# Sources of the first maxima and the order of the early expert rows in an attention and MoE kernel

## The chip, the cores and the metric

The kernel runs on one core of one Trainium2 chip. Times are device microseconds (us). A core has TensorE (PE in the profile, PEld its weight loads), VectorE (DVE), ScalarE (ACT), GpSimd (POOL) and SyncE (SP, here mostly the queue that issues transfers); GpSimd issues the indirect ones, gathers and scatters by a list of row numbers.

## The reference

Attention over 8 batches of 8 heads (576 positions, 64 per head) with a decay from a running sum of logarithms, then a mixture of 8 experts of which each row takes one:

```python
scores = scale * np.matmul(q, k.transpose(0, 1, 3, 2))
log_f = np.log(np.clip(f, 0.0001, 1.0))
cum = np.cumsum(log_f, axis=-1)
decay = cum[:, :, :, None] - cum[:, :, None, :]
scores = np.where(causal, -1000000000.0, scores + decay)
scores = scores - np.max(scores, axis=-1, keepdims=True)
attn = np.exp(scores)
attn = attn / (np.sum(attn, axis=-1, keepdims=True) + 1e-09)
x = np.matmul(attn, v)                      # then to rows of 512
...
logits = x @ w_gate
e_idx = np.argmax(logits, axis=1)
gate_w = softmax(logits)[e_idx]
eom = 1.0 / (1.0 + np.exp(-(x @ w_output_gate)))
out[e_idx == e] = gate_w * eom[:, e] * (np.maximum(x[e_idx == e] @ w1[e], 0.0) @ w2[e])
```

4608 rows of 512 go through W1 (512 x 1024) and W2 (1024 x 512) of their expert.

## The kernel before, in words

**Attention** is a program of steps, from -18 to 203, six steps for a unit of two heads; there are 32 units. A table, OFF, gives for each kind of work the step of a unit at which it is issued, and the engines run what they are given in that order. Before the exponent a unit needs the largest score of each row. maxsteps forms the scores of a block on TensorE, adds the decay there and reduces on VectorE into nR (L313); max_pair turns nR to half precision on ScalarE (mh, L374); max_turn transposes it on TensorE (mt, L379). The decay is a matmul of a few rows: Eq holds ones, Ek the running sum in three half-precision parts (few, L297). The running sum is made once for all 64 heads, in the prologue: a logarithm on ScalarE (L164), a scan and the parts on VectorE (tile d2, 64 partitions, one a head; the parts are cpc), and small DMAs that carry the parts of units 0 and 1 into Ek. wgs is the gate's weight, scaled on VectorE (L862). Vs holds V in a high and a low part, the low one by a subtraction (L143).

**Features.** The attention rows of two units each (u = 0 to 15 in feats) become x16 in two parts; DMA transposes bring them to xT (feats_turn, L568), from which TensorE makes the logits (route), and feats_out stores the rows in xbuf (L575, L580). route gives every row its place in its expert's list, and GpSimd scatters the row's number there, a tile of 128 rows at a time (tbl, L680): five scatters for the odd batches, four for the even.

**Experts.** The first 384 rows of experts 0 and 1 are taken early, those of expert 1 from batches 0 to 5: SyncE reads the row numbers (ids, L727), GpSimd gathers the rows (xg, L731), DMA transposes make xT (L737). up is xT times W1 (hp, L952), 8 pieces of 12 matmuls with 384 columns; down is the result times W2 (y, L980 to L982), a tile of 128 rows at a time, and each tile is scattered into the output by GpSimd (L985). The weights come as single-precision pieces (w1r, L693; w2r, L710) that are split into two parts, w1h on ScalarE and w1l on VectorE or GpSimd (L700), w2h and w2l likewise. Where attention ends TensorE does up and down of expert 0's early rows, batch 7's logits between the second and third tile of down, then expert 1's early rows (x1), then late rows and experts 2 to 7.

The semaphores of SyncE's transfers are eight that are used in turn.

Of the kernel before, what the change touches and what calls it, by code (L numbers as in the profile page):

```python
# [9 lines left out]
F32 = mybir.dt.float32  # L10
# [44 lines left out]
OFF = {'lead': 2, 'crow': -16, 'clear': 32, 'clearstep': 12, 'prefill': -15, 'fetch': -22, 'spread': -21, 'end': 204, 'max': (-15, -13, -11, -10), 'pair': -8, 'mturn': -7, 'rows': -6, 'put': -6, 'rscore': 2, 'rexp': 3, 'first': -9, 'av': ((6, 8, 8), (10, 10, 10)), 'fetch_v': -23, 'v': ((-15, -9, -17), (-9, 0, -12)), 'feats0': 20, 'feats1': 22, 'fturn': 21, 'fturnstep': 1, 'fout': 33, 'route': 46, 'rank': 6, 'w1r': [169, 170, 171, 175, 176, 178, 180, 181], 'w1': [174, 175, 178, 179, 181, 182, 200, 202], 'w2r': [183, 184, 184, 186, 186, 187], 'hold': (160, 196), 'ids1': 192, 'gather': 172, 'ids': 7, 'gturn': 6, 'route_last': 200, 'nsum': (9, 11), 'nrec': (10, 12), 'nx': (10, 13), 'nrest': (11, 14), 'mv': ['xr', 'v0', 'sm'], 'same': (-4, 0), 'begin': -18, 'pd': [7], 'turn': {'v0': 0, 'v1': 0, 'f0': 0, 'f1': 1, 'w': 1}, 'wg': -4, 'fetch_v/1': -15, 'dve': [172, 173, 181, 183, 184, 185, 186, 187, 189, 190], 'w1pool': [0, 1, 2, 3, 4, 5, 6, 7], 'order': 'nrec tick reduce rows v1 put spread fetch_v fout feats1 scores feats0 tick v0 max fetch exps mturn tick rexp nsum extra rscore av maxrest route fturn pair nx tick nrest', 'epool': [6, 7]}  # L55
# [11 lines left out]
def _attn_moe(ctx, tc, qk, vm, f, wg, w1, w2, out):  # L67
# [87 lines left out]
    def prologue():  # L155
# [34 lines left out]
    for t in (pick, negm, negt):  # L190
        nc.gpsimd.memset(t, 0.0)
    for i in range(HU):
        for h in range(2):
            def select(t, sign, op, fill):
# [92 lines left out]
    def maxsteps(u):  # L287
# [471 lines left out]
    def attention():  # L759
# [7 lines left out]
        for s in range(OFF["begin"], OFF["end"]):  # L767
# [82 lines left out]
            def extras():  # L850
# [5 lines left out]
                if s == OFF["ids1"]:  # L856
                    gather_ids(ar, tbl[NT:NT + EARLY], ET, 0, (st["ids"],))
# [40 lines left out]
        return [c for c in chains]  # L898
# [110 lines left out]
    with tc.manual_schedule(engines=ENGINES):  # L1009
# [37 lines left out]
        for _ in range(11):  # L1047
            next(chain)
# [127 lines left out]
```

## Time and profile before

| | us |
|---|---|
| timed, median of 3 | 799.69 |
| the 3 runs | 798.03 to 801.85 |
| profiled execution, own time | 792.31 |
| its span, first to last instruction | 790.6 |
| TensorE busy in the span | 753.9 (95%) |
| GpSimd, VectorE, ScalarE busy | 462.8, 355.0, 343.2 |
| mean granted TensorE clock | 0.99 |

All rows come from the one profiled execution. Busy time overlaps between engines. A timeline's row is an instruction, or a run of like ones (x8: eight), with the idle time of its engine before it and what ended that. For SyncE's queue a row's time is that of issuing, waits included, not of the transfer.

### The profile page before, as it was taken

What the parts mean: (1) busy time and instruction counts of PE and PEld (TensorE: products, weight loads), DVE (VectorE), ACT (ScalarE), POOL (GpSimd) and SP (SyncE); (2) the same over time, 40 slices, a digit from 0 to 9 for tenths busy, and PEclk for the clock granted to TensorE, in tenths of its full rate; (3) what the DMA queues carried; (4) which work ended last, traced back from release to release, by engine and by line L of the source; (5) the groups of instructions that cost most, each with busy time, mean ns of one, the idle gap of its engine ahead of it and who ended that gap; (6) DMA issues with size and microseconds to landing.
All of it is one profiled execution on the core that took longest, in us unless ns stands there. A gap on an engine that the chain in (4) does not pass through costs nothing. (4 is left out here: it accounts for less than half of the span.)

```text
span 790.6 us, 21337 instructions
## 1 busy us (share of the span) xinstructions
PE 753.9 (95%) x8677; PEld 493.5 (62%) x8695; DVE 355.0 (45%) x909; ACT 343.2 (43%) x821; POOL 462.8 (59%) x488
## 2 busy tenths in 40 slices
PE   4899999999989999899799999999999999999996
PEld 1577777777767777675355667556465574664752
DVE  7566687777767878976350142002011020120210
ACT  2556666465646564664331424333333333333211
POOL 9567669687867877656154538464564654736001
PEclk9999999999999999999989999999999999999999
DMA  5446678778867778599959739456562594452001
GB/s 189 135 126 149 178 186 184 185 174 172 159 166 165 174 193 184 115 217 187 209 114 259 201 86 260 130 167 152 174 162 75 175 210 129 139 118 80 11 13 45
DMA packets 136245, 121.49 MB, mean 154 GB/s; under 512 B 95342, under 2 KB 104974, under 8 KB 136144
## 3 DMA queue, kind: packets, MB, share of 16 engines
q1 hardware_dynamic: 128592, 101.18, 54.4%
q0 software_dynamic: 7552, 18.92, 7.7%
q8 instruction: 69, 1.13, 0.7%
q14 instruction: 32, 0.26, 0.1%
HBM read 81.63 MB, written 20.48 MB: 129 GB/s over the span
## 5 line engine op out<-in xcount | busy, mean ns | idle before, releaser
L415 POOL TENSOR_TENSOR plo<-p 128x512 f16<-128x512 f32 x167 | 173.4, 1054 | 62.7 <-ACT p L413 39.5
L962 DVE SCALAR_TENSOR_TENSOR hl<-hp,hh 128x384 f16<-128x384 f32 (+1 forms) x128 | 60.7, 491 | 304.2 <-ACT hh L961 179.9
L952 PE MATMUL hp<-xT,w1h 128*128 128x256 f16 (+1 forms) x1024 | 190.2, 302 | 5.4 <-DMA xT<-xg 5.4
L413 ACT ACTIVATE p<-sc 128x512 f32<-128x512 f32 x192 | 110.3, 593 | 67.3 <-PE sc L285 61.4
L285 PE MATMUL sc<-qk 64*128 64x64 f32 (+5 forms) x642 | 135.0, 476 | 0.0
L952 PEld LDWEIGHTS <-w1h 128*128 128x128 f16 x1024 | 100.6, 98 | 46.7 <-issue 7.5
L985 POOL DMA_INDIRECT out_dram<-ys,ids x40 | 40.2, 1005 | 144.0 <-ACT ys L984 87.6
L980 PE MATMUL y<-w2h,hh 128*128 128x512 f16 x320 | 121.9, 381 | 1.8 <-ACT w2h L912 1.8
L952 PE MATMUL hp<-xT,w1l 128*128 128x384 f16 (+1 forms) x512 | 122.9, 301 | 0.0
L982 PE MATMUL y<-w2h,hl 128*128 128x512 f16 x320 | 121.9, 381 | 0.9
L981 PE MATMUL y<-w2l,hh 128*128 128x512 bf16 x302 | 115.2, 382 | 0.3 <-DVE w2l L913 0.3
L961 ACT ACTIVATE hh<-hp 128x384 f16<-128x384 f32 (+1 forms) x128 | 50.8, 436 | 131.2 <-PE hp L952 120.1
L328 DVE CUSTOM_DVE_ANT_0 spare<-mx,wide 128x512 bf16<-128x512 f32 (+1 forms) x120 | 74.9, 624 | 43.1 <-PE mx L285 38.4
L984 ACT ACTIVATE ys<-y,ids 128x512 f32<-128x512 f32 x40 | 27.5, 687 | 152.6 <-issue 99.1
L700 POOL TENSOR_TENSOR w1l<-w1r,w1h 128x512 bf16<-128x512 f32 x54 | 61.8, 1158 | 50.5 <-ACT w1h L699 50.4
L285 PEld LDWEIGHTS <-pick 64*128 64x128 bf16 (+1 forms) x1152 | 59.2, 96 | 41.9 <-issue 24.6
L313 DVE TENSOR_REDUCE nR<-mx 128x1 f32<-128x576 f32 (+3 forms) x95 | 60.5, 637 | 29.1 <-PE mx L285 27.3
L489 PE MATMUL av<-Vs,p 128*128 128x65 f16 x640 | 70.4, 195 | 2.9 <-ACT xr L536 2.2
L285 PE MATMUL mx<-qk 64*64 64x64 bf16 (+2 forms) x374 | 59.3, 310 | 13.7 <-DMA qk<-in_qk_dram 8.6
L491 PE MATMUL av<-Vs,plo 128*128 128x65 f16 x640 | 69.3, 193 | 0.5 <-issue 0.5
L490 PE MATMUL av<-Vs,p 128*128 128x64 bf16 x640 | 69.8, 196 | 0.0
L952 PEld LDWEIGHTS <-w1l 128*128 128x128 bf16 x512 | 50.4, 98 | 20.1 <-issue 1.0
(166 smaller groups left out, 1430.8 us busy)
## 6 DMA issues: line engine op xcount, KB each, us to landing
qk<-in_qk_dram SPq DMA_DIRECT2D x32, 576.0 KB
w1r<-in_w_dram SPq DMA_DIRECT2D x64, 256.0 KB
w2r<-in_w_dram SPq DMA_DIRECT2D x64, 256.0 KB
v<-in_vm_dram SPq DMA_DIRECT2D x16, 576.0 KB
wide<-crow SPq DMA_DIRECT2D x30, 288.0 KB
xbuf<-x SPq DMA_DIRECT2D x16, 512.0 KB
Eq<-mts SPq DMA_DIRECT2D x64, 0.1 KB
xbuf<-x SPq DMA_DIRECT2D x16, 64.0 KB
```

What stands on the lines that cost most here:

```text
L285: nc.tensor.matmul(dst(i), w(i), x(i), start=start, stop=stop)
L328: nc.vector.tensor_tensor_reduce(out=spare[:, 0:n], in0=part(m, i, o, n), in1=t["wide"][:, i * S:i * S + n], scale=1.0, scalar=-3e38, op0= ...
L413: nc.scalar.activation(out=f32, in_=src, func=AF.Exp, scale=0.125)
L415: ins = eng.tensor_tensor(lo, f32, upper(f32), op=ALU.subtract)
L489: nc.tensor.matmul(dst, ph, vv[:, 0:W], start=kc == 0, stop=False)
L490: nc.tensor.matmul(dst[:, 0:D], ph, vv[:, W:].bitcast(BF16), start=False, stop=False)
L491: nc.tensor.matmul(dst, pl, vv[:, 0:W], start=False, stop=kc == qc)
L700: ins = (eng or nc.vector).tensor_tensor(l, raw, h, op=ALU.subtract)
L952: nc.tensor.matmul(m[:, 0:(t1 - t0) * P], w[:, k], xT[:, t0:t1, k // 2, j, k % 2], start=k == 0 and i == 0, stop=k == ND - 1 and i == 2)
L980: nc.tensor.matmul(y, hh[:, fc, sl], wh, start=fc == 0, stop=False)
L981: nc.tensor.matmul(y, hh[:, fc, sl], wl, start=False, stop=False)
L982: nc.tensor.matmul(y, hl[:, fc, sl], wh, start=False, stop=fc == NF - 1)
```

## The change

In the start: for units 0 and 1 the decay's stationary operand is a column of the identity, spread, and its moving operand the first part of the running sums of all heads (cpa, 128 partitions, of which the upper 64 are zeroed), so that a column picks its head. Ek of units 0 and 1 is filled with ones by ScalarE, two memsets go to VectorE, the loads have another order on SyncE, the low part of V (V's first two subtractions) and the gate's scaling stand at later steps.

Where attention ends: the features of u = 15 are transposed on TensorE and copied from PSUM (feats_swap); batch 7's logits come right behind up, its ranks behind the first tile of down; the numbers of expert 1's rows are read after all scatters of batch 5, and batch 6's scatters stand ahead of expert 1's gathers; expert 2's gathers stand between splits of W1.

```diff
-OFF = { ... 'v': ((-15, -9, -17), (-9, 0, -12)), ... 'wg': -4, ... }
+OFF = { ... 'v': ((-15, -9, -5), (-9, 0, -3)), ... 'wg': 20, ... }
...
@@ -79,10 +79,12 @@
     d1 = ar.tile([P, 2048], F32, name="d1", tag="x")[0:B * H]
-    d2 = ar.tile([P, 2048], F32, name="d2", tag="x")[0:B * H]
+    d2f = ar.tile([P, 2048], F32, name="d2", tag="x")
+    d2 = d2f[0:B * H]
     ft, lf, zr = [d1[:, j * S:(j + 1) * S] for j in range(3)]
     cum, rem = [d2[:, j * S:(j + 1) * S] for j in range(2)]
     cpc = d2[:, 2 * S:2 * S + 3 * S // 2].bitcast(F16).rearrange("p (c s) -> p c s", c=3)
+    cpa = d2f[:, 2 * S:2 * S + S // 2].bitcast(F16)
     raw = {}
...
@@ -112,7 +114,7 @@
         return slice(i * D, (i + 1) * D)
     def blank(i, eng=nc.gpsimd):
-        if i != 1:
+        if i > 1:
             eng.memset(Eks[i], 1.0)
         eng.memset(Eqs[i], 0.0)
...
@@ -156,9 +158,11 @@
         nc.sync.dma_start(ft, f)
         fetch(0)
-        nc.sync.dma_start(wg32, wg)
-        fetch_v(0)
+        fetch(1)
         nc.vector.memset(zr, 0.0)
+        for i in range(2):
+            nc.scalar.activation(out=Eks[i].rearrange("p (n q) -> p n q", q=D), func=AF.Copy, scale=0.0, bias=1.0,
+                                 in_=identh[:, 0:D].unsqueeze(1).broadcast_to([P, S // D, D]))
         blank(0, nc.vector)
         nc.vector.tensor_scalar(ft, ft, 1e-4, 1.0, op0=ALU.max, op1=ALU.min)
         nc.scalar.activation(lf, ft, AF.Ln)
...
@@ -173,8 +177,9 @@
             for u in range(2):
                 nc.sync.dma_start(Eks[u].rearrange("(h d) s -> h d s", h=HU)[:, i, :],
                                   cpc[u * HU:(u + 1) * HU, i, :])
-        fetch(1)
+        fetch_v(0)
         fetch(2)
+        nc.sync.dma_start(wg32, wg)
     order = actx.enter_context(ExitStack())
...
@@ -182,23 +187,18 @@
     wg32 = cp.tile([P, 4, 2 * E], F32, name="wg32")
     late = cp.tile([P, EE], F32, name="late")
+    apart = cp.tile([P, 1], F32, name="apart")
     identh = cp.tile([P, P], F16, name="identh")
-    nc.gpsimd.memset(Eks[1], 1.0)
     make_identity(nc, identh)
+    nc.gpsimd.memset(cpa[B * H:], 0.0)
...
+        (nc.gpsimd if t is negt else nc.vector).memset(t, 0.0)
...
@@ -294,13 +294,20 @@
         def few(x, i, sl):
-            return x[i * D:i * D + 1 if u < 2 else (i + 1) * D - 1, sl]
+            return x[i * D:(i + 1) * D - 1, sl]
+        def own(i, n):
+            return identh[:, HU * u + i:HU * u + i + 1].broadcast_to([P, n])
         def block(m, o, c):
             n = (c + 1) * P
             q = slice(c * P, n)
-            decay = [(lambda i: part(m, i, o, n), lambda i: few(t["Eq"], i, q), lambda i: few(t["Ek"], i, slice(0, n)),
-                      False, False)]
+            if u < 2:
+                decay = [(lambda i: part(m, i, o, n), lambda i: own(i, P), lambda i: cpa[:, 0:n], False, False)]
+            else:
+                decay = [(lambda i: part(m, i, o, n), lambda i: few(t["Eq"], i, q),
+                          lambda i: few(t["Ek"], i, slice(0, n)), False, False)]
...
@@ -356,10 +363,10 @@
             m = mtile().rearrange("p b n -> p (b n)")[:, 0:S]
             q = slice(SM, S)
             for sl in (slice(0, SM), q):
-                own = sl is q
+                last = sl is not q
                 heads([(lambda i: m[rows(i), sl], lambda i: Qu[rows(i), q], lambda i: Ku[rows(i), sl], True, False),
-                       (lambda i: m[rows(i), sl], lambda i: few(t["Eq"], i, q), lambda i: few(t["Ek"], i, sl),
-                        False, not own)])
+                       (lambda i: m[rows(i), sl], lambda i: own(i, SR) if u < 2 else few(t["Eq"], i, q),
+                        lambda i: cpa[:, sl] if u < 2 else few(t["Ek"], i, sl), False, last)])
...
@@ -853,8 +860,6 @@
                 for e in range(EE):
                     if s == OFF["hold"][e]:
                         hold_early(e)
-                if s == OFF["ids1"]:
-                    gather_ids(ar, tbl[NT:NT + EARLY], ET, 0, (st["ids"],))
                 if s == OFF["gather"]:
                     chains.append(early_gather())
@@ -895,7 +900,15 @@
             for name in OFF["order"].split():
                 todo[name]()
             assert set(todo) == set(OFF["order"].split())
-        return [c for c in chains]
+        for c in chains[:-1]:
+            n = len(scatters)
+            while next(c, c) is not c:
+                now[0] += 1
+                if len(scatters) > n:
+                    nc.gpsimd.memset(apart, 0.0)
+                    n = len(scatters)
+        gather_ids(ar, tbl[NT:NT + EARLY], ET, 0, (st["ids"],))
+        return chains[-1:]
...
@@ -1006,6 +1019,18 @@
     x1 = (st["ids"], m2.tile([P, CT, 2, 2, DM // P // 2, P], F16, name="xT", bufs=1))
     first = [(0, ET)]
     late_rows = [(ET, CT)]
+    def feats_swap(u, t0, copy):
+        xT, x16 = xTs[u]
+        t1 = min(t0 + 2, NTB)
+        n = (t1 - t0) * 4
+        m = pm.tile([P, DM], F32, name="y", bufs=2).bitcast(F16).rearrange("p (c n) -> p c n", n=P)
+        src = x16[:, t0:t1].rearrange("p t j (k n) -> p (t j k) n", n=P)
+        for c in range(n):
+            nc.tensor.transpose(m[:, c], src[:, c], identh)
+        copy(out=xT[:, t0:t1].rearrange("p t j k n -> p (t j k) n"), in_=m[:, 0:n])
     with tc.manual_schedule(engines=ENGINES):
         for t in range(ET):
             gather_rows(x1, t, EARLY_B[1] * S, (ET + t) % CT)
@@ -1021,9 +1046,9 @@
             if fc == 1:
                 for part in range(2):
                     feats(NQ - 1, part)
-                    for t in ((0,), (2, 4))[part]:
-                        feats_turn(NQ - 1, t)
                 feats_out(NQ - 1)
+            if fc in (4, 5, 6):
+                feats_swap(NQ - 1, 2 * (fc - 4), nc.scalar.copy if fc == 5 else nc.vector.tensor_copy)
         W1r = [fetch_w1(m2, w1[1], fc, 8) for fc in range(NF)]
         for t in range(ET):
             gather_turn(x1, t, (ET + t) % CT)
@@ -1038,14 +1063,13 @@
             if len(raws) < NF:
                 raws.append(fetch_w2(w2[e], len(raws)))
-        down(W2, x, h, 0, 2)
-        more_w1(2, nc.vector)
         for _ in range(9):
             next(chain)
-        more_w1(2, nc.vector)
-        down(W2, x, h, 2, ET)
+        down(W2, x, h, 0, 1)
         for _ in range(11):
             next(chain)
+        more_w1(4, nc.vector)
+        down(W2, x, h, 1, ET)
         for t, _ in enumerate(chain):
             if t % 2:
                 more_w1(1, nc.gpsimd)
...
@@ -1067,12 +1091,12 @@
         x2 = next_ids(ar, EE)
         W1r = [fetch_w1(m2, w1[EE], fc, 8) for fc in range(NF)]
         W2r = [fetch_w2(w2[EE], fc) for fc in range(6)]
-        for t in range(CT):
-            gather_rows(x2, t)
         down(W2b, x1, h, 0, ET)
         W1c = []
         for fc in range(NF):
             up_split(up_products(W1, x, late_rows, fc), h, late_rows, fc)
+            if fc < CT:
+                gather_rows(x2, fc)
             W1c.append(split_w1(ar, W1r[fc], NF, nc.gpsimd))
         x2 = next_turns(ar, x2)
         down(W2, x, h, ET, CT)
```

VectorE, from the first reduction of the program. Vs is the low part of V, nR the maxima of unit 0, mts the transposed maxima. Before:

```order
L313 TENSOR_REDUCE nR<-mx 128x2
L313 TENSOR_REDUCE nR<-av 128x1 x4
L143 TENSOR_TENSOR Vs_90<-v_153,Vs_90 128x9x64
L313 TENSOR_REDUCE nR<-sc 128x1 x2
L313 TENSOR_REDUCE nR<-mx 128x1
```

After:

```order
L320 TENSOR_REDUCE nR<-mx 128x2
L320 TENSOR_REDUCE nR<-av 128x1 x4
L320 TENSOR_REDUCE nR<-sc 128x1 x2
L320 TENSOR_REDUCE nR<-mx 128x1
L394 COPY mts<-mt 9x128
```

The subtraction has left the middle of unit 0's reductions; it stands behind those of unit 1 now.

GpSimd, where attention ends. tbl with pi_7856 (after: pi_7858) are batch 5's scatters, with pi_8660 (pi_8663) batch 6's; xg are expert 1's gathers. Before:

```order
L700 TENSOR_TENSOR w1l_8592<-w1r_8142,w1h_8591 128x512
L680 DMA tbl_202<-rec_222,pi_7856 36864x2 x2
L731 DMA xg_226<-xbuf_73,ids_7804 128x1024 x3
L680 DMA tbl_202<-rec_222,pi_8660 36864x2 x4
L985 DMA out_0_dram<-ys_8923,ids_7801 4608x512
```

After:

```order
L700 TENSOR_TENSOR w1l_8593<-w1r_8144,w1h_8592 128x512
L687 DMA tbl_204<-rec_224,pi_7858 36864x2
L908 MEMSET apart_101 128x1
L687 DMA tbl_204<-rec_224,pi_7858 36864x2
L687 DMA tbl_204<-rec_224,pi_8663 36864x2 x4
L738 DMA xg_228<-xbuf_73,ids_7806 128x1024 x3
L998 DMA out_0_dram<-ys_9004,ids_7803 4608x512
```

The gathers have moved behind batch 6's scatters, and a small memset stands between the last two of batch 5.

SyncE there, with the semaphores that each instruction waits for (DMAHW0 to 7 are those of SyncE's own transfers, DMASW those of GpSimd's). Before:

```order
L568 DMA_TRANSPOSE xT_8334<-x_8335 128x8x128 [waits DMAHW3_49,DVE_49]
L727 DMA ids<-tbl 128x3x2 [waits DMAHW4_49,DMASW3_49]
L568 DMA_TRANSPOSE xT_8334<-x_8335 128x4x128 [waits DMAHW5_49,DVE_49]
L575 DMA xbuf<-x_8335 128x4x512 [waits DMAHW6_49]
L580 DMA xbuf<-x_8335 64x512 [waits DMAHW7_49]
L580 DMA xbuf<-x_8335 64x512 [waits DMAHW0_49]
L710 DMA w2r<-in_w_dram 128x512 [waits DMAHW1_49,DVE_49]
L710 DMA w2r<-in_w_dram 128x512 [waits DMAHW2_49,DVE_49]
L568 DMA_TRANSPOSE xT_8739<-x_8740 128x8x128 [waits DMAHW3_49,DVE_49,PE_49]
L568 DMA_TRANSPOSE xT_8739<-x_8740 128x8x128 [waits DMAHW4_49,DVE_49]
L568 DMA_TRANSPOSE xT_8739<-x_8740 128x4x128 [waits DMAHW5_49,DVE_49]
L575 DMA xbuf<-x_8740 128x4x512 [waits DMAHW6_49]
```

After:

```order
L575 DMA_TRANSPOSE xT_8336<-x_8337 128x4x128 [waits DMAHW4_49,DVE_49]
L582 DMA xbuf<-x_8337 128x4x512 [waits DMAHW5_49]
L587 DMA xbuf<-x_8337 64x512 [waits DMAHW6_49]
L587 DMA xbuf<-x_8337 64x512 [waits DMAHW7_49]
L717 DMA w2r<-in_w_dram 128x512 [waits DMAHW0_49,DVE_49]
L734 DMA ids<-tbl 128x3x2 [waits DMAHW1_49,DMASW5_49]
L717 DMA w2r<-in_w_dram 128x512 [waits DMAHW2_49,DVE_49]
L582 DMA xbuf<-x_8743 128x4x512 [waits DMAHW3_49,DVE_49]
L587 DMA xbuf<-x_8743 64x512 [waits DMAHW4_49,DVE_49]
L587 DMA xbuf<-x_8743 64x512 [waits DMAHW5_49]
L700 DMA w1r<-in_w_dram 128x512 [waits DMAHW6_49,Pool_49]
```

The read of ids has moved from between the transposes of u = 14 to between the last two pieces of W2, and waits for a later scatter; the three transposes of xT_8739 (u = 15) are gone.

## Rows read from the trace of the kernel before

**Rows 1.** Windows: span, busy (count) of PE, PEld, DVE, ACT, POOL; granted clock, DMA, GB/s.

```profile
0.00:20.00 20.00, 9.70 (x75) 3.67 (x76) 14.87 (x31) 4.92 (x7) 18.05 (x54) 1.00 0.58 189
...
420.00:780.00 360.00, 359.21 (x2177) 214.24 (x2191) 56.96 (x124) 115.86 (x244) 175.21 (x161) 1.00 0.50 139
```

**Rows 2.** Timeline of VectorE, first 24 us: start, us, engine, line, operation [idle before].

```profile
9.69 1.23 DVE L313 TENSOR_REDUCE nR<-mx 128x2 f32<-128x1024 f32 x1 [0.26 <-PE mx L285]
...
11.28 1.42 DVE L313 TENSOR_REDUCE nR<-av 128x1 f32<-128x384 f32 x4 [0.37 <-PE av L285]
...
12.62 0.75 DVE L143 TENSOR_TENSOR Vs<-v,Vs 128x576 bf16<-128x576 f32 x1
...
19.62 0.18 DVE L862 TENSOR_SCALAR wgs<-wg 128x64 f16<-128x64 f32 x1
...
19.98 0.68 DVE L313 TENSOR_REDUCE nR<-mx 128x2 f32<-128x512 f32 x1
```

**Rows 3.** Timeline of ScalarE, the same stretch.

```profile
0.83 1.28 ACT L164 ACT_TABLE_LOAD   x1 [0.83 <-PEq L1164]
...
4.48 0.68 ACT L164 ACTIVATE d<-d 64x576 f32<-64x576 f32 x1 [2.37 <-DVE d L163]
...
14.73 0.21 ACT L374 ACTIVATE mh<-nR 128x9 f16<-128x9 f32 x1 [5.50 <-DVE nR L313]
```

**Rows 4.** Timeline of TensorE, start of the program.

```profile
8.74 0.61 PE L285 MATMUL mx<-Ek,Eq 1*128 1x512 f16 x2 [2.58 <-DMA Ek<-d]
...
20.71 0.63 PE L285 MATMUL mx<-qk 64*64 64x512 bf16 x2 [1.65 <-DVE nR L313]
...
28.05 0.22 PE L379 MATMUL mt<-identh,mh 128*9 128x128 f16 x1
```

**Rows 5.** Timeline of TensorE where attention has ended.

```profile
376.85 0.38 PE L980 MATMUL y<-w2h,hh 128*128 128x512 f16 x1 [1.83 <-ACT w2h L912]
...
396.61 0.80 PE L952 MATMUL hp<-xT,w1h 128*128 128x384 f16 x2 [5.25 <-DMA xT<-xg]
...
402.19 0.49 PE L952 MATMUL hp<-xT,w1h 128*128 128x384 f16 x2
```

**Rows 6.** Windows of 5 us over the same place, columns as in group 1.

```profile
375.00:380.00 5.00, 2.82 (x9) 1.09 (x9) 1.20 (x2) 1.68 (x3) 0.83 (x1) 0.81 1.22 172
380.00:385.00 5.00, 5.00 (x25) 2.20 (x24) 0.00 (x0) 0.00 (x0) 0.17 (x1) 0.84 0.99 104
...
395.00:400.00 5.00, 3.39 (x11) 1.61 (x12) 0.00 (x0) 0.07 (x1) 4.10 (x5) 0.52 0.92 301
```

**Rows 7.** Timeline of SyncE's queue (SP), 340 to 445 us.

```profile
363.58 4.49 SPq L568 DMA_TRANSPOSE xT<-x  x3
...
370.53 17.06 SPq L693 DMA_DIRECT2D w1r<-in_w_dram  x8
...
387.69 5.77 SPq L737 DMA_TRANSPOSE xT<-xg  x3
...
410.96 0.89 SPq L727 DMA_DIRECT2D ids<-tbl  x2
```

**Rows 8.** Timeline of GpSimd (POOL), 340 to 445 us.

```profile
354.95 2.27 POOL L700 TENSOR_TENSOR w1l<-w1r,w1h 128x512 bf16<-128x512 f32 x2 [3.69 <-ACT w1h L699]
...
361.69 1.48 POOL L680 DMA_INDIRECT tbl<-rec,pi  x1 [4.47 <-DMA ids<-tbl]
...
364.76 1.54 POOL L731 DMA_INDIRECT xg<-xbuf,ids  x1 [0.30 <-issue]
...
391.00 0.99 POOL L985 DMA_INDIRECT out_dram<-ys,ids  x1 [10.84 <-issue]
...
396.66 0.98 POOL L680 DMA_INDIRECT tbl<-rec,pi  x1 [0.30 <-issue]
...
403.88 0.98 POOL L680 DMA_INDIRECT tbl<-rec,pi  x1 [0.17 <-issue]
...
413.73 1.04 POOL L731 DMA_INDIRECT xg<-xbuf,ids  x1 [6.57 <-DMA ids<-tbl]
```

More of the change, by code (lines that the diff above doesn't have):

```diff
@@ L51 @@
 EE = 2
-OFF = {'lead': 2, 'crow': -16, 'clear': 32, 'clearstep': 12, 'prefill': -15, 'fetch': -22, 'spread': -21, 'end': 204, 'max': (-15, -13, -11, -10), 'pair': -8, 'mturn': -7, 'rows': -6, 'put': -6, 'rscore': 2, 'rexp': 3, 'first': -9, 'av': ((6, 8, 8), (10, 10, 10)), 'fetch_v': -23, 'v': ((-15, -9, -17), (-9, 0, -12)), 'feats0': 20, 'feats1': 22, 'fturn': 21, 'fturnstep': 1, 'fout': 33, 'route': 46, 'rank': 6, 'w1r': [169, 170, 171, 175, 176, 178, 180, 181], 'w1': [174, 175, 178, 179, 181, 182, 200, 202], 'w2r': [183, 184, 184, 186, 186, 187], 'hold': (160, 196), 'ids1': 192, 'gather': 172, 'ids': 7, 'gturn': 6, 'route_last': 200, 'nsum': (9, 11), 'nrec': (10, 12), 'nx': (10, 13), 'nrest': (11, 14), 'mv': ['xr', 'v0', 'sm'], 'same': (-4, 0), 'begin': -18, 'pd': [7], 'turn': {'v0': 0, 'v1': 0, 'f0': 0, 'f1': 1, 'w': 1}, 'wg': -4, 'fetch_v/1': -15, 'dve': [172, 173, 181, 183, 184, 185, 186, 187, 189, 190], 'w1pool': [0, 1, 2, 3, 4, 5, 6, 7], 'order': 'nrec tick reduce rows v1 put spread fetch_v fout feats1 scores feats0 tick v0 max fetch exps mturn tick rexp nsum extra rscore av maxrest route fturn pair nx tick nrest', 'epool': [6, 7]}
+OFF = {'lead': 2, 'crow': -16, 'clear': 32, 'clearstep': 12, 'prefill': -15, 'fetch': -22, 'spread': -21, 'end': 204, 'max': (-15, -13, -11, -10), 'pair': -8, 'mturn': -7, 'rows': -6, 'put': -6, 'rscore': 2, 'rexp': 3, 'first': -9, 'av': ((6, 8, 8), (10, 10, 10)), 'fetch_v': -23, 'v': ((-15, -9, -5), (-9, 0, -3)), 'feats0': 20, 'feats1': 22, 'fturn': 21, 'fturnstep': 1, 'fout': 33, 'route': 46, 'rank': 6, 'w1r': [169, 170, 171, 175, 176, 178, 180, 181], 'w1': [174, 175, 178, 179, 181, 182, 200, 202], 'w2r': [183, 184, 184, 186, 186, 187], 'hold': (160, 196), 'ids1': 192, 'gather': 172, 'ids': 7, 'gturn': 6, 'route_last': 200, 'nsum': (9, 11), 'nrec': (10, 12), 'nx': (10, 13), 'nrest': (11, 14), 'mv': ['xr', 'v0', 'sm'], 'same': (-4, 0), 'begin': -18, 'pd': [7], 'turn': {'v0': 0, 'v1': 0, 'f0': 0, 'f1': 1, 'w': 1}, 'wg': 20, 'fetch_v/1': -15, 'dve': [172, 173, 181, 183, 184, 185, 186, 187, 189, 190], 'w1pool': [0, 1, 2, 3, 4, 5, 6, 7], 'order': 'nrec tick reduce rows v1 put spread fetch_v fout feats1 scores feats0 tick v0 max fetch exps mturn tick rexp nsum extra rscore av maxrest route fturn pair nx tick nrest', 'epool': [6, 7]}
 MV = OFF['mv']
@@ L184, in _attn_moe @@
     late = cp.tile([P, EE], F32, name="late")
+    apart = cp.tile([P, 1], F32, name="apart")
     identh = cp.tile([P, P], F16, name="identh")
-    nc.gpsimd.memset(Eks[1], 1.0)
     make_identity(nc, identh)
+    nc.gpsimd.memset(cpa[B * H:], 0.0)
     pick, negm, negt = [cp.tile([P, 2, P], BF16, name=n) for n in ("pick", "negm", "negt")]
[L190 to L194, printed above, removed]
+    for t, sign, op, fill in ((pick, 1, ALU.not_equal, 1.0), (negm, 1, ALU.is_ge, -8e9), (negt, -1, ALU.is_ge, -8e9)):
+        (nc.gpsimd if t is negt else nc.vector).memset(t, 0.0)
+        for i in range(HU):
+            for h in range(2):
                 nc.gpsimd.affine_select(out=t[rows(i), h], in_=t[rows(i), h], pattern=[[-sign, P]], compare_op=op,
                                         fill=fill, base=sign * h * D, channel_multiplier=sign)
-            select(pick, 1, ALU.not_equal, 1.0)
-            select(negm, 1, ALU.is_ge, -8e9)
-            select(negt, -1, ALU.is_ge, -8e9)
     prologue()
```

## The prediction

> **What bounds the kernel now.** I read the busy times by engine first, then windows over the whole core, then the timeline of TensorE for its idle stretches. TensorE is the bound nearly everywhere: from 420 to 780 us it is busy 359.21 of 360 us [rows 1], so nothing that the change moves there can pay unless it starts earlier. Two places are left. In the first 20 us TensorE is busy 9.70 us [rows 1], since the decay and the first maxima pass through one chain from engine to engine. [...] The reader is to see that these two hold all that can be gained, and that everything else counts only by delaying them.
>
> The sum is made against the profiled execution, 792.31 us; the timed median, 799.69, lies 7.4 above it, and I carry that difference over.
>
> **The start.** The headline edit takes the decay of the first two units' maxima out of Ek. TensorE's first such matmuls stand at 8.74 us behind a wait of 2.58 for the DMA into Ek [rows 4]. That wait is mostly not on the path: the reduction which reads them, at 9.69, waited for TensorE only 0.26 us; VectorE had been busy till then with the sums that make the decay [rows 2]. So at most 0.26 goes. Against it stands a new load on ScalarE: two fills of Ek ahead of the logarithm, which I price at 0.68 each, as the logarithm over the same 576 columns, and an activation table more, 1.28 [rows 3]. From 0.83 that is 1.28 + 2 x 0.68 + 1.28, the logarithm at 4.75 instead of 4.48: 0.27 later. The first part comes out at nothing, and 0.7 worse if the first fill waits for the identity that GpSimd builds.
>
> What does pay is what leaves VectorE's chain. The subtraction for V, 0.75 at 12.62, stood between two reductions of the first unit, of which one waited 0.37 for TensorE [rows 2]; it goes behind both units. I count 0.7 and 0.37. The gate's two scalings, from 19.62 to 19.98, 0.36 us, stood before the reduction for which TensorE waits 1.65 at 20.71 [rows 2, 4]; they go to step 20, where TensorE is the bound. The sum is -1.4. Below it the term ends at -2.9 (the whole wait of 1.65 and the pieces that ScalarE's 14.73 ends [rows 3] with it), above it at +0.3, if a load on SyncE's queue that now stands behind other ones (V and the gate) is late.
>
> **The end of attention.** Three moves work on one chain there, that of expert 1's early rows: numbers (ids1), gathers, transposes, then TensorE.
>
> What holds it now: the scatters of batch 5 end late since scatter 4 waits 4.47 us for SyncE's read of the numbers [rows 8], and expert 1's transposes stand behind eight reads of W1, 17.06 us long, at 387.69 [rows 7]; xT is ready at 396.61, 8.9 us after the first of these is issued. The length of the 17.06 is from semaphores that must come back: each transfer waits for the one eight before it, and three of those are transposes of the last features (4.49 us of the queue, at 363.58).
>
> Now scatter 4 needs no wait: it follows the split at 354.95 + 2.27 = 357.2, scatter 5 at 358.7 (1.48 each). Its landing isn't in the trace. Batch 7's five took from 396.66 to 410.96, 14.3 us or 2.86 each, and the last 7.1 from its own issue [rows 7, 8]. Two from 357.2 make 362.9, 7.1 from 358.7 makes 365.8: I take these as ends, with the whole 14.3 as a far end (a rival). A read of numbers takes 2.8 (410.96 to 413.73). So batch 6's four scatters start at 365.7 to 368.6, are issued 1.5 apart, and at 2.86 each have landed by 377 to 380. The gathers follow at about 372 to 375 and land with or behind them. SyncE reaches the W1 reads at 366 to 370, and now without the three transposes among those waited for; the last three wait for the features' stores, which I expect behind the scatters, at 377 to 380. Then 8.9 us for the transposes: xT at 386 to 389. If nothing but the 4.49 is saved it is 392.1; if nothing at all, 396.6. I take 390, near the first.
>
> TensorE itself: it would be done at 396.61 - 5.25 = 391.36. The wait of 1.83 for W2's last piece goes, because matmuls of 128 columns, logits and ranks now stand between up and down and the three transposes that shared the DMA engines with that piece are gone; cover lost, its 1.83 stays. With no pause before it the clock doesn't fall: 375 to 385 had 0.81 and 0.84 granted [rows 6], 0.95 + 0.80 = 1.75. To this come 20 transposes of 128 columns. The one transpose of the trace takes 0.22 at the low clock [rows 4], 4.4 in all; a matmul at 420 to 780 takes 359.21/2177 = 0.165 with 256 columns or more [rows 1], so 0.08 each, 1.6 in all, which I take as the nearer row. Their copies lie on VectorE and ScalarE, which are half idle there (1.20 and 1.68 busy of 5 us [rows 6]). TensorE is free at 391.36 - 1.83 - 1.75 + 1.6 = 389.4.
>
> [...]
>
> So expert 1's up starts at 390 instead of 396.61: -6.6. From 396.61 to 402.19 it ran at the low level (0.52 granted from 395 to 400; two matmuls took 0.80, then 0.49 [rows 5, 6]); 5.58 us of work at half speed, 2.8 lost. Without a wait of several microseconds before it that is back: -2.8.
>
> The added cost is GpSimd's. The splits of W1 4 to 7 for expert 1 stand there behind the out scatters and among batch 7's scatters, 396.66 to 404.9 now [rows 8]. If up starts 6.6 earlier these must too. An out scatter waited 10.84 for the one before (at 391.00); with the other scatters earlier in the queue I expect most of it gone, and count +1.0 (0 to +4).
>
> Expert 2's gathers, placed between splits, cost nothing by the 359.21 of 360: TensorE covers them; uncovered, a gather's 1.54 would show once [rows 8]. The two memsets that VectorE takes over at the very start lie in ScalarE's wait of 2.37 for the numbers f [rows 3]; uncovered they delay the whole chain by their own few tenths.
>
> Sum: -1.4 - 6.6 - 2.8 + 1.0 = -9.8: 782.5 in the profiled execution's terms, 789.9 or 790.0 beside the median.
>
> **The rivals.**
> 1. *The numbers earlier, the rows not.* The eight W1 reads keep their 17.06 and xT comes at 396.6 as now; the pause stays and with it the low clock. For it: SyncE's queue is in order, the same DMA engines carry scatters, W1 and rows (104 GB/s at 380 to 385 [rows 6]). Against: three of the eight transfers waited for are gone. Only -1.4 is left: 798.3.
> 2. *GpSimd's chain of outs takes over.* Each out still waits some 10 us for the former, batch 7's scatters stay at 396.66, the last splits end at 407 as now. Up reaches its eighth piece at 390 + 7 x 1.98 = 403.9 (12 matmuls a piece at the 0.165 above) and waits 3.2 there, 1.0 of which is counted; that the last two splits (2.27) follow scatter 403.88 [rows 8] is where the 407 is from. 782.5 + 2.2, beside the median 792.1.
> 3. *Slower: SyncE stands at the read of expert 1's numbers.* The read waits for batch 5's last scatter and everything behind it on SyncE (the last piece of W2, the stores, W1, the transposes) waits along. If that scatter lands 14.3 after its issue, at 373.0, the numbers are there at 375.8, and W1's reads begin 5.3 after 370.53; 17.06 and 8.9 behind make xT 401.9. With the start's gain lost to the logarithm (+0.3): 797.9, beside the median 805.3. It decides from a landing later than 370.5 on, 11.8 after the issue. For it speaks the 14.3; against it that those were five scatters and here there are two.
> 4. *The transposes on TensorE are dear.* Each takes the 0.22 of [rows 4], 4.4 in all, and the clock stays low while they run, so the 1.75 isn't won: TensorE is free at 391.36 - 1.83 + 4.4 = 393.9, 3.9 after the 390 of the sum: 793.8. For it: the only row of a transpose; against it: that row stands among half-clock matmuls. [...]
>
> **How the numbers follow.** Forecast 0.56, rival 1 0.17, rival 2 0.15, rival 3 0.07, rival 4 0.05. No change is within 0.5% of 799.69, 4.0 us, which is about what a measurement of this kernel can tell: 795.7 to 803.7. The forecast and rivals 2 and 4 are faster, 0.76; rival 1 is the same, 0.17; rival 3 slower, 0.07. The forecast's own range is 785.5 to 793 (start -2.9 to +0.3, xT from 386 to 392, splits 0 to 4, not all at one end). To leave out no more than 2 in 10, the range goes over rivals 2 and 4 to rival 1: 785.0 to 798.5.
>
> **What would show it.** Right: the pause before expert 1's up under 2 us, no stretch of half clock behind it, TensorE's first exponent matmuls 1 to 2 us earlier, the transposes under 2 us in sum. Wrong at the start: VectorE's first reduction later than 10.0. Rival 1: the read of W1 still 17 us on SyncE's queue and the transposes at 387. Rival 2: a wait of TensorE for w1l inside expert 1's up. Rival 3: SyncE still at the numbers after 370. Rival 4: a granted clock under 0.9 with the transposes in it.

## The result

Before, the kernel took 798.03 us (median of 5 runs, 793.34 to 801.85); changed, it took 788.06 (5 runs, 781.26 to 792.60): a ratio of 0.986, 95% interval 0.982 to 0.991. Measured once more on another chip the ratio was 0.994 (0.988 to 0.999). Ratios count only fast executions, without those more than 1.5% above the fastest of their kernel; on the second chip the fast ones average 790.0 before and 784.4 changed. It is faster, by 0.6 to 1.4%. Forecast were 790.0 and a step of 9.8 us; the step is 10.0 on the first chip and 5.7 on the second. The span of the profiled execution went from 790.6 to 779.6, an own time of 781.26.

### The profile after

Windows of the changed kernel over the stretches of [rows 1, 6] (columns as there); between them the stretch in which expert 1's up starts:

```profile
0.00:20.00 20.00, 11.05 (x79) 3.89 (x79) 14.26 (x29) 6.88 (x9) 17.83 (x52) 0.91 0.59 192
375.00:380.00 5.00, 4.19 (x25) 1.75 (x24) 3.95 (x19) 3.10 (x8) 1.03 (x1) 1.00 0.87 131
380.00:385.00 5.00, 4.95 (x23) 2.25 (x23) 1.40 (x3) 0.88 (x2) 1.01 (x1) 1.00 0.92 218
385.00:390.00 5.00, 5.00 (x28) 2.64 (x27) 0.00 (x0) 2.20 (x5) 0.98 (x1) 1.00 1.00 307
```

TensorE is busier at both places, and at the end of attention the granted clock stays at 1.00 where it was 0.52 to 0.84 [rows 6]. The first row can't be held against the 1.00 of [rows 1] in the same way: there the matmuls of 512 columns take 0.61 to 0.64 us, the time of the lower level, as the start's experiments show below, so that 1.00 is no measure of the level that TensorE ran at.

The start on VectorE, to be held against [rows 2]:

```profile
9.55 1.21 DVE L320 TENSOR_REDUCE nR<-mx 128x2 f32<-128x1024 f32 x1
...
10.76 1.42 DVE L320 TENSOR_REDUCE nR<-av 128x1 f32<-128x384 f32 x4
12.09 0.75 DVE L320 TENSOR_REDUCE nR<-sc 128x1 f32<-128x256 f32 x2
12.89 0.76 DVE L320 TENSOR_REDUCE nR<-mx 128x1 f32<-128x576 f32 x1
```

on ScalarE, against [rows 3]:

```profile
2.12 1.25 ACT L164 ACTIVATE Ek<-identh 128x576 f16<-128x576 f16 x2
...
4.68 0.68 ACT L168 ACTIVATE d<-d 64x576 f32<-64x576 f32 x1
...
13.68 0.21 ACT L381 ACTIVATE mh<-nR 128x9 f16<-128x9 f32 x1 [6.80 <-DVE nR L320]
```

and on TensorE, against [rows 4]:

```profile
7.38 1.01 PE L285 MATMUL mx<-d,identh 128*128 128x512 f16 x2 [1.22 <-POOL negt L200]
...
11.66 0.41 PE L285 MATMUL mx<-qk 64*64 64x512 bf16 x2
...
19.48 0.41 PE L285 MATMUL mx<-qk 64*64 64x512 bf16 x2 [1.07 <-DVE nR L320]
```

The wait for Ek is gone and the first reduction comes only 0.14 sooner, as VectorE's sums end then; the logarithm is 0.20 later. The half precision maxima come 1.05 sooner. One row was not expected: the matmuls at 11.66 and 19.48 take 0.41, where the one at 20.71 took 0.63 before [rows 4].

The end of attention on TensorE, against [rows 5]; L1031 are the transposes, L650 the ranks, L965 with w1h at 387.60 the first of expert 1:

```profile
359.81 0.61 PE L1031 MATMUL y<-identh,x 128*128 128x128 f16 x8
360.25 0.49 PE L965 MATMUL hp<-xT,w1h 128*128 128x384 f16 x2
...
362.20 0.61 PE L1031 MATMUL y<-identh,x 128*128 128x128 f16 x8
362.65 0.49 PE L965 MATMUL hp<-xT,w1h 128*128 128x384 f16 x2
...
364.60 0.39 PE L1031 MATMUL y<-identh,x 128*128 128x128 f16 x4
364.82 0.49 PE L965 MATMUL hp<-xT,w1h 128*128 128x384 f16 x2
...
368.24 0.38 PE L993 MATMUL y<-w2h,hh 128*128 128x512 f16 x1 [0.31 <-issue]
369.69 0.38 PE L995 MATMUL y<-w2h,hl 128*128 128x512 f16 x1 [1.08 <-issue]
...
372.57 0.39 PE L995 MATMUL y<-w2h,hl 128*128 128x512 f16 x1 [0.33 <-issue]
...
377.07 0.19 PE L650 MATMUL rk<-oh,before 128*128 128x40 bf16 x1 [0.62 <-DVE oh L636]
...
387.60 0.49 PE L965 MATMUL hp<-xT,w1h 128*128 128x384 f16 x2
...
400.12 0.34 PE L965 MATMUL hp<-xT,w1l 128*128 128x384 f16 x1 [0.34 <-POOL w1l L707]
```

Expert 1's up follows down without a pause and at the upper level (two matmuls 0.49, 1.00 granted from 385 to 390), 9.0 us sooner than at 396.61 [rows 5], of which 4.67 is the whole attention being sooner. In the first tile of down stand pauses put down to "issue", 2.5 us in sum with the shorter ones, that weren't there before.

The chain that feeds it, on SyncE's queue (against [rows 7]) and on GpSimd (against [rows 8]):

```profile
360.99 0.38 SPq L734 DMA_DIRECT2D ids<-tbl  x1
...
364.75 3.89 SPq L700 DMA_DIRECT2D w1r<-in_w_dram  x8
380.78 4.07 SPq L744 DMA_TRANSPOSE xT<-xg  x3
```

```profile
353.71 0.97 POOL L687 DMA_INDIRECT tbl<-rec,pi  x1 [0.19 <-issue]
365.43 0.97 POOL L687 DMA_INDIRECT tbl<-rec,pi  x1 [10.74 <-DMA ids<-tbl]
...
370.52 1.05 POOL L738 DMA_INDIRECT xg<-xbuf,ids  x1 [0.30 <-issue]
...
373.20 1.01 POOL L738 DMA_INDIRECT xg<-xbuf,ids  x1 [0.30 <-issue]
...
383.99 1.01 POOL L998 DMA_INDIRECT out_dram<-ys,ids  x1 [5.50 <-ACT ys L997]
...
390.10 0.97 POOL L687 DMA_INDIRECT tbl<-rec,pi  x1 [0.30 <-issue]
```

The eight reads of W1 take 3.89 of the queue instead of 17.06. Expert 1's gathers are issued from 370.52 to 374.2 and its transposes follow from 380.78, 6.6 us behind; W1's reads, done with the queue at 368.6, no longer stand before them.

### The profile page after: what moved, and what is told of

The parts are those of the page before. It is cut to its first block, busy times and chain, and to the rows that moved or that the text cites. A ratio compares the mean times of both kernels' runs of the same rounds, so it can differ in the third digit from the quotient of the medians.

```text
span 779.6 us, 21385 instructions
## 1 busy us (share of the span) xinstructions
PE 748.8 (96%) x8697; PEld 490.5 (63%) x8715; DVE 357.1 (46%) x912; ACT 346.7 (44%) x825; POOL 461.0 (59%) x487
## 5 line engine op out<-in xcount | busy, mean ns | idle before, releaser
L965 PE MATMUL hp<-xT,w1h 128*128 128x256 f16 (+1 forms) x1024 | 188.2, 299 | 0.8 <-issue 0.5
L285 PE MATMUL sc<-qk 64*128 64x64 f32 (+5 forms) x642 | 133.2, 471 | 0.0
L965 PEld LDWEIGHTS <-w1h 128*128 128x128 f16 x1024 | 99.9, 98 | 40.8 <-DMA xT<-xg 0.8
L965 PE MATMUL hp<-xT,w1l 128*128 128x384 f16 (+1 forms) x512 | 121.9, 299 | 0.3 <-POOL w1l L707 0.3
L496 PE MATMUL av<-Vs,p 128*128 128x65 f16 x640 | 69.7, 194 | 3.2 <-ACT xr L543 1.6
L965 PEld LDWEIGHTS <-w1l 128*128 128x128 bf16 x512 | 50.1, 98 | 20.1 <-POOL w1l L707 0.7
```

Source lines behind the costliest of these rows:

```text
L285: nc.tensor.matmul(dst(i), w(i), x(i), start=start, stop=stop)
L496: nc.tensor.matmul(dst, ph, vv[:, 0:W], start=kc == 0, stop=False)
L965: nc.tensor.matmul(m[:, 0:(t1 - t0) * P], w[:, k], xT[:, t0:t1, k // 2, j, k % 2], start=k == 0 and i == 0, stop=k == ND - 1 and i == 2)
```

## The experiments

All profiles are measured by the same marks, read from the timelines: the first exponent, the start of expert 0's up, the wait of TensorE for xT before expert 1's up, and the stretch from the start of expert 0's up to that of the late rows, which holds the whole end of attention.

| kernel | first exponent | expert 0's up | wait for xT | stretch |
|---|---|---|---|---|
| before | 25.10 | 354.61 | 5.25 | 75.8 |
| after | 22.06 | 349.94 | 0 | 69.7 |
| changed_again | 25.19 | 349.97 | 5.04 | 71.5 |
| e1_start | 23.93 | 351.80 | 7.91 | 77.9 |
| e2_end | 25.09 | 353.38 | 1.51 | 70.6 |
| e3_column | 29.38 | 355.99 | 0 | 72.2 |
| e4_vwg | 24.59 | 352.68 | 4.64 | 75.0 |
| e9_column_alone | 25.70 | 350.61 | 6.18 | 77.8 |
| e6_logits_late | 25.18 | 349.84 | 1.50 | 68.8 |
| e6_again (the same kernel) | 23.74 | 358.34 | 4.64 | 71.0 |
| e7_spread | 23.86 | 353.44 | 4.95 | 72.4 |
| e8_ids_early | 25.20 | 360.01 | 4.62 | 72.9 |
| e10_ids_only | 22.97 | 355.58 | 6.84 | 72.1 |
| e11_six_on_dve | 22.01 | 353.06 | 1.74 | 66.6 |

From the first exponent to expert 0's up hardly an edit stands (the gate's scaling, 0.36 us on VectorE, has moved there), and yet this part varies from 324.7 (e6_logits_late) to 334.8 us (e8_ids_early) between executions. So the total of one execution proves little here, and the stretch is the better witness. It varies too: by 1.8 between after and changed_again and by 2.2 between e6_logits_late and e6_again, which are each one kernel twice.

### The two halves apart

e1_start is the start's edits on the kernel before, e2_end the end's:

```diff
 # e1_start: loads, fills, few/own, V and gate steps as changed; the rest as before
 # e2_end: ids behind the scatters, feats_swap, logits first, x2's gathers between splits; the rest as before
```

> The change's start alone, the end of attention as before. Theory A (start and end are independent, the start is worth what the first exponent shows, 25.10 to 22.06): first exponent at 22.1, every later step up to the last exponents 3.4 us earlier than before, and the pauses before expert 1's rows (1.83 and 5.25) as before; about 3.4 us faster, 0.4%. Rival B (the start's gain is given back at transfers that come no sooner, as the query loads in the middle of attention): first exponent at 22.1, but expert 0's up within 1 us of where it was; within 1 us of the kernel before.

> The change's end of attention alone, the start as before. Theory A: 6 to 8 us faster (0.8 to 1.0%), expert 1's up within 1 us behind the end of down and at full clock, first exponent at 25.1. Rival B (the end's gain needs the earlier start, since batch 5's scatters and the read of numbers run against a fixed clock): a wait of 2 us or more for xT, half clock behind it, 3 to 5 us faster. Both kernels tell whether TensorE stalls in the first tile of down (some 3 us, in steps of 1.43 us, in the changed kernel) come with the new order: theory C (the new order causes them) expects them here again, rival D (chance of that one execution) does not.

Measured: e1_start 0.998 (0.995 to 1.001), no difference that can be told; e2_end 0.993 (0.990 to 0.996). In e1_start the first exponent came 1.17 sooner, not 3.0, and at the second unit it was 0.97; the stretch stayed long. In e2_end the clock stayed up (two matmuls 0.48 behind the wait), but TensorE still waited 1.51 for xT, and 0.7% is a little under the 0.8 to 1.0 expected. Theory A holds in the main for the end and misses the size for the start: what the times can tell of the change is its end. Multiplied, the halves make 0.991, between the two ratios of the whole. The stalls come again in e2_end and e3_column (2.7 and 3.1 us); see below.

### What pays at the start

```diff
 # e3_column, from the changed kernel
-'v': ((-15, -9, -5), (-9, 0, -3)), ... 'wg': 20
+'v': ((-15, -9, -17), (-9, 0, -12)), ... 'wg': -4
 # e4_vwg, from the kernel before: the same two keys the other way
 # e9_column_alone, from e1_start: these two keys and the order of the loads as before
```

> The changed kernel with V's subtraction and the gate's scaling back at their former steps, so the identity column and the load order alone at the start. Theory A (what paid was VectorE's chain): maxima of unit 0 turned at 14.7 as before, first exponent at 24 or later. Rival B (the identity column pays, by shorter pauses on TensorE and full clock sooner): first exponent at 22.1 to 23.3, matmuls of 512 columns at 0.4 instead of 0.6 us before 24.

> The kernel before with V's subtraction and the gate's scaling at the steps of the change, nothing else. Theory A (VectorE's chain): first exponent 1.4 us or more sooner, 23.7 or less, the half precision maxima at 13.7 instead of 14.73. Rival B (the column is needed): first exponent at 24.5 to 25.1, since TensorE still waits for Ek.

> The change's identity column alone (with the fills on ScalarE and the memsets on VectorE), loads in the former order, V's subtraction and the gate's scaling at their former steps, the end of attention as before. Theory A (VectorE's sums bound the first reduction): first reduction at 9.7, half precision maxima at 14.4 to 15.0, first exponent 24.5 to 25.3 if TensorE's matmuls of 512 columns take 0.6 us up to there; 22.5 or less only where they take 0.4 from 12 us on. Rival B (the column alone pays): maxima at 13.9 or less and first exponent at 24.1 or less with 0.6 us matmuls.

e4_vwg: maxima 0.14 sooner, first exponent 0.51, and at the second unit 0.02 later: VectorE's shorter chain alone is worth nothing. e9_column_alone: maxima 0.29 sooner, first exponent 0.60 later: nor is the column alone. e3_column is a warning: V is now loaded behind the six transfers into Ek, so its subtraction at the old step holds the maxima until 18.13, and the first exponent is 4.28 later. The moves belong together. What decides in the nine profiles with the whole changed start is in these rows of TensorE at the same place (same columns as above), before first, then e1_start, then e7_spread:

```profile
12.00 0.64 PE L285 MATMUL mx<-qk 64*64 64x512 bf16 x2
```

```profile
11.68 0.64 PE L284 MATMUL mx<-qk 64*64 64x512 bf16 x2
```

```profile
11.68 0.41 PE L285 MATMUL mx<-qk 64*64 64x512 bf16 x2
```

With 0.64 there (e1_start, e6_logits_late, e8_ids_early, changed_again) the maxima come 0.43 sooner and the second unit's exponents 0.97 sooner to 0.15 later; with 0.41 (after, e6_again, e7_spread, e11_six_on_dve) the maxima come 1.0 to 1.2 sooner and those exponents 1.34 to 3.41 (e10_ids_only, where the level rises between 12 and 14, 2.61).

That 0.41 and 0.64 are the two levels of the clock shows in e3_column: its granted clock is 0.96 from 10 to 15 us and 0.50 from 15 to 30, and the same matmul takes 0.41 in the first stretch (at 11.50) and 0.64 in the second (at 24.97). In e7_spread it takes 0.41 at 11.68 and 0.64 at 19.45; in after the granted clock is 1.00 from 11.7 to 14.9 us, 0.50 from 15.2 to 18.4 and 1.00 again from 19.4 to 25.0. So the level can fall again, and the gain goes with how long it is up before the first exponent: 10.4 us in e11_six_on_dve (first exponent 3.09 sooner than before), 7.1 in after (3.04) and in e10_ids_only (2.13), 6.8 in e6_again (1.36), 3.4 in e7_spread and e1_start (1.24 and 1.17), and not at all in changed_again, e6_logits_late and e8_ids_early (0.08 to 0.10 later). In e9_column_alone and e3_column it was up by 12 us too, but down behind waits of 2.19 and 5.70 us for the maxima (the transpose there took 0.27 in both, 0.22 in after), and the first exponent came later than before.

In the three profiles without the column (before, e2_end, e4_vwg) TensorE takes 0.64 at 12 us each time. So the start's gain goes with when and how long TensorE is at its upper level, and that differs between executions of the same start. With the column, TensorE was there by 12 us in six of eleven profiles and without it in none of three; that the column makes it likelier is suggested, not shown.

### The logits' place, and the stalls

```diff
 # e6_logits_late: the order of down, logits, ranks and W1 splits as before
 # e7_spread: route yields after each row tile's 8 logit matmuls, and
+            for _ in range((0, 0, 0, 0, 0, 2, 2, 1)[fc]):
+                next(chain)                     # behind pieces 5, 6, 7 of up
```

> The changed kernel with batch 7's logits, its ranks and the splits of W1 0 to 3 back at their former places among the tiles of down (the transposes on TensorE and the later read of numbers stay). Theory E (the stalls of 2.5 to 3.1 us come where the 40 short logit matmuls run while GpSimd issues its chain of four scatters and three gathers): the first tile of down takes 5.2 us, no pause of 0.3 or more in it except for a piece of W2, and expert 1's up then waits 1.5 to 3 us for xT, since that lands no sooner; total within 0.3% of the changed kernel. Rival F (the stalls belong to the transposes or to the first tile of down itself): pauses of the same sum at the same place.

> The changed kernel with the 40 logit matmuls split in three groups (16, 16, 8) behind pieces 5, 6 and 7 of up, the rest of the order as changed. Theory E: groups this short cause no stall or less than 0.8 us in sum, VectorE's reduction of the logits follows within 1 us, and a wait for xT takes the stall's place: total within 0.3% of the changed kernel. Rival F: 2.5 to 3.1 us of stalls in the first tile of down again. Rival G (GpSimd's chain holds VectorE, whatever TensorE does): no stall on TensorE, but the reduction still comes 1.3 us behind the end of the chain.

> The changed kernel once more, unaltered, for its second profile. What is repeatable of its parts: the first exponent 0 to 3 us sooner than before (where TensorE's matmuls of 512 columns take 0.4 us early on, 1 us or more; else at most 0.6), the stretch from the start of expert 0's up to the late rows 3.5 to 6.1 us shorter. Theory E' (stalls behind the 40 logits belong to their new place): 2 us or more in the first tile of down; rival I (they are chance, they also came once at the old place): less than 1 us or none.

> The kernel with late logits, unaltered, beside the changed one on the same chip. Theory E': 0 to 1.5 us faster than the changed kernel (the stalls of 2.5 to 3.1 us gone, 1.5 of them back as a wait for xT); rival I: the same within 0.3%.

e6_logits_late: no pause in the first tile of down, then 1.50 for xT, as theory E had it; on its chip 0.992 (0.988 to 0.995) of before. e7_spread: no pause either, 4.95 for xT; 0.989 (0.985 to 0.993). But the unaltered changed kernel in its second profile had none:

```profile
388.71 0.80 PE L965 MATMUL hp<-xT,w1h 128*128 128x384 f16 x2 [5.04 <-DMA xT<-xg]
```

and e8_ids_early none with the 40 logits right among GpSimd's indirect transfers. So theories E and E' have fallen, F too (changed_again has the transposes and the order); rival I, chance, is what is left. Stalls of 2.5 to 3.1 us came in three of the five profiles with all logits first. Shorter pauses for "issue", 0.78 us in sum, stand in the first tile of down of e1_start as well, which has the old order and no logits there; the pause of 1.57 among the logits of e9_column_alone is put down to the DMA of xT and is another matter. Why TensorE pauses there is open; no run tells it. Their cost is small: after and changed_again begin expert 0's up at the same time (349.94 and 349.97), and expert 1's at 387.60 with the stalls and at 388.71 without, since there TensorE waits for xT instead. Run side by side, the late logits (e6_again, 0.992, 0.988 to 0.997) and the changed kernel (0.994, 0.988 to 0.999) can't be told apart, and the late logits' second profile waited 4.64 for xT, not 1.50: that the logits come sooner is worth nothing that can be measured.

### What brings the rows sooner

```diff
 # e8_ids_early, from the changed kernel: the read of numbers at step 192 and the gathers first, as before
 # e10_ids_only, from e6_logits_late: the last features' three DMA transposes as before, no feats_swap
```

> The changed kernel with the read of expert 1's numbers back at its former step, so that the gathers go ahead of batch 6's scatters (only the numbers' source is older; logits first and transposes on TensorE stay). Theory A (the rows came sooner because the read of numbers no longer holds scatter 4 and 5 and the gathers follow): xT 3 us or more later than in the changed kernel. Rival H (the rows came sooner because the three transposes of the last features are gone from SyncE's queue): xT as soon or sooner, at or before the end of down, no wait of TensorE before expert 1's up.

> The changed kernel with the last features transposed by DMA again and the logits late, so that at the end of attention only the later read of numbers, the scatters ahead of the gathers and expert 2's gathers are left of the change. Theory A (the read of numbers moved is what brings the rows sooner): the stretch from the start of expert 0's up to the late rows 5 us or more shorter than before, TensorE waits less than 3 us for xT. Rival H (the three DMA transposes must go as well): less than 3 us shorter, W1's reads 12 us or more on SyncE's queue and a wait for xT of 4 us or more.

SyncE's queue in e10_ids_only:

```profile
367.34 4.13 SPq L575 DMA_TRANSPOSE xT<-x  x3
373.82 9.91 SPq L700 DMA_DIRECT2D w1r<-in_w_dram  x8
386.35 5.52 SPq L744 DMA_TRANSPOSE xT<-xg  x3
```

Each edit alone leaves a wait of 4.6 and 6.8 us; with both it was 0 to 5.0 (mean of after, changed_again, e2_end, e3_column 1.6), against 4.6 to 7.9 in the four profiles with the old end (mean 6.0). The stretches: 72.9 and 72.1 for one, 71.0 on average for those four with both, 76.6 on average for none (before, e1_start, e4_vwg, e9_column_alone).

The wait also depends on when TensorE is done, so it doesn't tell when the rows came. Counted from the start of expert 0's up, expert 1's up got its rows at 41.1 to 44.4 us with the old end, at 38.3 in e8_ids_early, at 39.4 in e10_ids_only, and at 35.2 to 38.7 in the six profiles with both edits in which TensorE waited (changed_again and e2_end 38.7). So either edit alone brings the rows some 2 to 6 us sooner, and what the second adds is within what one kernel varies (35.2 in e6_logits_late, 38.3 in e6_again). Theory A fails on e8_ids_early, where it expected the rows 3 us later: the gathers are issued 10.2 us behind the start of expert 0's up there, against 20.6 in the changed kernel, the transposes at 21.9 against 30.8, but they take 13.50 of the queue instead of 4.07, and the rows are no sooner and no later than in changed_again. Its stretch is 1.5 longer than that of changed_again by two waits for GpSimd's splits (0.97 and 0.49), not by the rows. Rival H fails on its wait of 4.62. In e10_ids_only the wait of 6.84 is as H had it; the stretch, 3.7 shorter than before, lies between the two theories, and the reads of W1 are shorter than H's 12.

The reads of W1 take 12.0 to 17.1 of the queue with the old end, 9.91 and 9.01 with one edit, 3.9 to 7.7 with both. Of the 17.06 before, the profile puts 2.1 down to the transposes of the last features; the longest hold is another, from the fifth read, issued by 376.3, to the sixth, at 385.88, and by the order of the semaphores in the list of SyncE's instructions the sixth waits for that of the features' first store. So the transposes can't have held the queue by their own semaphores alone; that they also delayed the stores is likely, not shown. What the old read of numbers costs directly is the wait of scatter 4 (5.00 in e8_ids_early).

### A further step

```diff
 # e11_six_on_dve, from e6_logits_late
-        more_w1(2, nc.vector)
+        more_w1(4, nc.vector)
         down(W2, x, h, 2, ET)
```

> The kernel with late logits, and VectorE taking six of the eight W1 splits of expert 1 instead of four. If the splits on GpSimd are what is left there (1.64 and 0.48 us of waits for w1l inside expert 1's up), these waits go: 1 to 2 us faster than with late logits alone, 0.1 to 0.3%. Rival: batch 7's scatters come no later without the splits between them and nothing is gained, or the ranks wait for VectorE (1.3 us more in front of them) and the third tile of down ends later: within 0.1%.

In e6_logits_late expert 1's up waited for GpSimd's splits:

```profile
396.90 0.34 PE L965 MATMUL hp<-xT,w1l 128*128 128x384 f16 x1 [1.64 <-POOL w1l L707]
399.50 0.34 PE L965 MATMUL hp<-xT,w1l 128*128 128x384 f16 x1 [0.48 <-POOL w1l L707]
```

In e11_six_on_dve TensorE's only wait from 380 to 402 us is the one for xT:

```profile
388.48 0.49 PE L965 MATMUL hp<-xT,w1h 128*128 128x384 f16 x2 [1.74 <-DMA xT<-xg]
```

Its stretch is the shortest, 66.6, 2.2 less than e6_logits_late, which is about the sum of the two waits (2.12). In e6_again, however, the same kernel as e6_logits_late had no such waits, so the gain rests on one pair of profiles. Timed it is 0.988 of before (0.979 to 0.997), beside 0.992 of late logits alone: better in the profile, not proven better by the times.

## Why the prediction was right, and where its terms were not

The time was right to 2 us on the first chip, in part by luck: on the second the step was 5.7, not 9.8. Its terms were less right. By the sum's own steps, in the profiled executions:

- **The column is worth nothing in itself**: right. The logarithm came at 4.68 (4.75 said), the first reduction 0.14 sooner (nothing said).
- **The start, -1.4**: the mechanism was missed. I counted VectorE's pieces, which alone give nothing (e4_vwg). Measured was -3.04 at the first exponent in this execution, from +0.1 to -3.1 in the nine, by how long TensorE was at its upper level before it. The step that failed is "what does pay is what leaves VectorE's chain".
- **xT at 390**: mis-sized. Scatter 5 to the read took 7.3 (353.71 to 360.99; I had 4.2 to 7.1), the read to the first scatter 4.4 (2.8 said), the scatters 1.27 apart (1.5). xT was there by 387.60; as expert 0's up began 4.67 sooner, that is at most 392.3 in the old frame. In changed_again, where TensorE waited for it, it came at 393.3 in that frame, 3.3 later than I said and beyond the 386 to 392 of the range. 396.6 would have been rival 1.
- **TensorE free at 389.4**: 392.3 in the same frame, mis-sized by the 2.5 us of stalls and 0.62 for the ranks, which I had not priced: "logits and ranks now stand between up and down" was booked as cover, and cost. In changed_again, without stalls, it was 388.3.
- **The 20 transposes, +1.6**: they took 0.44 + 0.45 + 0.22 = 1.1 us (360.25 less 359.81, and so on) at a granted clock of 1.00, 55 ns each in a row, so rival 4 is out. The 0.22 of [rows 4] was read wrongly: it is the time of one transpose by itself, and not at the lower level, where the same transpose of the kernel before took 0.27:

```profile
15.00 0.27 PE L379 MATMUL mt<-identh,mh 128*9 128x128 f16 x1 [1.23 <-ACT mh L374]
```

- **So -6.6 was -4.34** (9.01 less 4.67) in this execution, and the -2.8 for the clock was -2.5: the rows behind expert 1's up come 11.15 sooner, 2.14 more than its start, with the 0.34 for a split in it. In changed_again the two were -3.3 and -1.1: behind the 5.04 of wait the level fell (two matmuls 0.80), and the sign given for "right", a pause under 2 us and no half clock behind it, did not hold.
- **+1.0 for the splits**: 0.34, and from 0 (changed_again) to 2.12 (e6_logits_late) in other profiles. Another 0.42 went between there and the late rows (10.73 sooner); 0.26 of it is a wait of TensorE for the late rows' xT at 419.67. Rival 2's out scatter waited 5.50, not 10.84, but 9.04 in changed_again.
- The remaining 1.6 of the 10.7 at the late rows came within attention, where hardly an edit stands. It is chance, as the table shows, and it covered the end's shortfall: the end gave 6.1 of the 8.4 that I had for it (75.8 less 69.7), 4.3 in changed_again, and 5.6 on the mean of four profiles.
- **Rival 3** did not come: SyncE left the read of numbers at 361.4.

## What to carry to other kernels

When a row of transfers is slow, look which semaphore each waits for: the 17.06 us fell to 9 or 10 with one edit and to 3.89 with both, while the transfers stayed the same, and more than half of it was one wait. Here a wait of TensorE for data was followed by the lower clock (5.25 us, then 0.52 granted from 395 to 400 [rows 5, 6]), and without it the rows behind expert 1's up gained 2.14 us beyond its earlier start, so the last microseconds of that wait were worth more than they looked; but first find what is late next, which here was GpSimd's splits. Where unedited parts vary by 10 us between executions, judge an edit by the stretch that holds it and by several profiles.

## What the runs showed that I had not expected

TensorE's matmuls of 512 columns took 0.41 or 0.64 us at the same place of the same start from one execution to the next (11.3 to 11.7 us, nine profiles; after and changed_again differ, and so do e6_logits_late and e6_again), and how long the upper level was held carried up to 3 us into the rest. TensorE paused for "issue" 2.5 to 3.1 us in steps of about 1.4 us among or behind 40 short matmuls in three of the five executions that have all logits first, and not in the other two.

A wait of 1.5 to 1.7 us before expert 1's up left the level up (0.48 or 0.49 for two matmuls in e2_end, e6_logits_late and e11_six_on_dve). The waits of 4.95 to 6.84 us there were followed by the lower level at the first two matmuls (0.80) in before [rows 5], changed_again, e7_spread and e10_ids_only. In e8_ids_early, behind 4.62, it came some 0.4 us later, and two matmuls then took 0.85:

```profile
398.33 0.48 PE L959 MATMUL hp<-xT,w1h 128*128 128x384 f16 x2 [4.62 <-DMA xT<-xg]
398.65 0.40 PE L959 MATMUL hp<-xT,w1l 128*128 128x384 f16 x1
398.85 0.85 PE L959 MATMUL hp<-xT,w1h 128*128 128x384 f16 x2
```
